# Windowed attention and two feed-forward layers on one core: granule 0's softmax normalized inside its transposition, and the opening planned anew

## The chip, the core and the metric

The kernel runs on one core of a Trainium2 chip. Its time is the device time of one execution in microseconds (us). The core's engines are TensorE (PE in the profile; PEld is its loading of weights), VectorE (DVE), ScalarE (ACT), GpSimd (POOL) and SyncE (SP), which here issues all the transfers (DMA).

## What is computed

The reference, cut to its core: attention for 2 batches of 8 heads, 768 tokens and 64 dimensions a head, in which a token sees its neighbours closer than 16 and 24 block summaries, then two feed-forward layers on the 1536 tokens.

```python
scores_l = scale * np.matmul(q, k.transpose(0, 1, 3, 2))     # only |i - j| < 16 is kept
scores_s = scale * np.einsum('bhsd,bhnd->bhsn', q, k_sum) + np.log(block)
a = np.exp(scores_all - np.max(scores_all, axis=-1, keepdims=True))
a = a / (np.sum(a, axis=-1, keepdims=True) + 1e-09)
attn_out = np.matmul(a, np.concatenate([v, v_sum], axis=2))  # k_sum: block max, v_sum: block mean
x = attn_out as [1536, 512]
h = x @ w_in;  x = (h * np.tanh(softplus(h))) @ w_out        # 512 -> 2048 -> 512
out = ((x @ w_a) * (x @ w_b)) @ w_out2                       # 512 -> 1536 -> 512
```

## The kernel before

The tokens are cut into six granules of 256, three to a batch. Heads are worked on in pairs (`p` 0 to 3, NP = 4), two heads side by side on the 128 partitions. For a granule and a pair the attention goes through these steps.

- `load_k`, `load_q`, `load_windows` and `prep_v` issue the transfers of keys, queries and values (all at L364); `prep_k` takes the block maxima of the keys on DVE (L462).
- `batch_s` makes the scores on PE: windows (L567, 64x96) and block summaries (L571, 64x24).
- `weights` is the softmax. DVE adds the mask and takes the minimum (L588, four times a pair), ACT takes the exponential with its sum (L594, four times), DVE adds 1e-9 (L597), takes the reciprocal (L599), and multiplies the 128x480 weights by it (L601).
- `batch_o` turns the weights over on PE (L626, four transpositions a pair), copies them out of PSUM on ACT or DVE (`copy`, L377 and L378; 120x512) and multiplies by the values (L638). Granule 0 alone adds the block values by a product of its own (L651), since its block means (L492, in `prep_v`, copied by `keep_v`) come late. The result is split into a rounded part (a CAST at L377 or L378) and a rest (L668).

The first feed-forward layer is done in `step1` for the first four chunks of 128 hidden units: `x_product` (L897), the activation Mish on ACT (L927), a rounded copy and a rest (L930 on DVE), and the product with `w_out` (L944). It starts on granule 0 while the other granules are still in the attention. All products of this kernel are made of three products of rounded parts. A chunk's weights come as 512 KB of 64-bit numbers and are converted by `load_w`: L688 on ACT, L693 and L696 on DVE, a CAST on ACT (L377) and the rest on DVE (L708). Later come the remaining chunks (L1076, L1121) and the second layer (L1076, L1229), which the change doesn't touch in the code.

No engine's order is written out. Every step is recorded in `Plan` by `Plan.add` with a key (the time at which it is due), the engines that may run it with a planned cost, and what it reads and writes. `Plan.emit` then plays the program through in planned time: at each moment each engine takes, of the steps whose inputs are there, the one with the smallest key; ACT adds `TABLE_PENALTY` to a step that needs another activation table than the one loaded (exp and Mish lie in different tables), PE adds `SHAPE_PENALTY` to a step whose products have another shape. The order so found is what each engine runs, and at run time each engine keeps it. So constants that only describe time (costs, due times, the model of the transfers) move instructions.

One more step has no part in the result: while PE has nothing to do early on, the plan puts in `fill`, a 128x512 bf16 product on zeros (L434) which keeps PE at work; eight stand at the start, and up to planned time `fill_end` more of them fill gaps. Once planned they run whether there is a gap or not.

## Time and profile before

| | us |
|---|---|
| median of 3 runs (lowest, highest) | 595.39 (595.28, 595.61) |
| the profiled execution | 595.54 |
| its span in the profile | 593.8 |

| engine | busy us | share of the span |
|---|---|---|
| PE | 586.6 | 99% |
| DVE | 489.2 | 82% |
| ACT | 318.8 | 54% |
| POOL | 6.7 | 1% |

The span runs from the first instruction to the last; 1.7 us of the profiled execution lie around it. The shares are means over stages: PE is busy throughout, DVE and ACT are nearly full from about 24 to 80 us and have slack afterwards. Times within the span are given from its start. The granted clock is the share of TensorE's full clock (2.4 GHz) that was granted in a stretch; its other level is half of that (1.2 GHz).

### The profile page before, as it was taken

The page shows a single profiled execution, that of the slowest core. Times are in us where ns is not written, and L with a number is a line of the kernel's source. Part 1 is how long each engine was busy: PE and PEld are TensorE (multiplying, and loading weights), DVE is VectorE, ACT ScalarE, POOL GpSimd, SP SyncE. Part 2 cuts the span into 40 slices and gives each one's busy share as a digit, 9 for nine tenths or more (in the row PEclk, how much of TensorE's full clock was granted, in tenths as well). Part 3 has the DMA queues.
Part 4 walks back from the last instruction along what each step waited for, and adds up shares of the span by engine and source line. Part 5 has one row for each costly group of instructions (what it writes and reads, how often), then busy time and mean ns, then how long its engine had stood idle before and what let it go on. Part 6 is the DMA issues. An engine that isn't in the chain of part 4 may idle for free.

```text
span 593.8 us, 10770 instructions
## 1 busy us (share of the span) xinstructions
PE 586.6 (99%) x4162; PEld 530.9 (89%) x4163; DVE 489.2 (82%) x1134; ACT 318.8 (54%) x711; POOL 6.7 (1%) x34
## 2 busy tenths in 40 slices
PE   9999999999999999999999999999999999999998
PEld 5788788889898899989999999999898999999896
DVE  6899999999999988979799998858686876855443
ACT  5699999457555555455376655444262434433030
POOL 3000000000000000000000000000000000000000
PEclk9899999999999999999999999999999999999999
DMA  9997700222233221222003133230122212300202
GB/s 282 348 345 221 224 20 3 71 72 72 71 107 106 73 71 72 72 71 72 0 1 100 43 107 111 103 107 20 52 72 71 108 35 72 107 0 2 89 18 107
DMA packets 22288, 54.89 MB, mean 92 GB/s; under 512 B 1917, under 2 KB 8061, under 8 KB 22237
## 3 DMA queue, kind: packets, MB, share of 16 engines
q1 hardware_dynamic: 22236, 54.21, 27.8%
q8 instruction: 32, 0.52, 0.4%
q14 instruction: 20, 0.16, 0.1%
HBM read 50.07 MB, written 3.15 MB: 90 GB/s over the span
## 4 chain that ended last, share of the span: by engine, by line
PE 92%; ACT 3%; DVE 3%; DMA 1%; issue 1%; ACTq 0%
PE bank L1076 44%; PE bank L1121 17%; PE bank L1229 17%; PE bank L944 5%; PE bank L897 4%; ACT attn L594 2%; PE bank L567 1%; PE bank L638 1%; DMA attn<-attn 1%; PE bank L626 1%; PE bank L434 1%; DVE attn L588 1%; ACT L927 1%; ACT rounded L377 0%; PE bank L571 0%
## 5 line engine op out<-in xcount | busy, mean ns | idle before, releaser
L1076 PE MATMUL bank<-rounded,wext 128*128 128x384 f32 x1176 | 213.8, 335 | 0.0
L1076 PEld LDWEIGHTS bank<-rounded,wext 128*128 128x128 f32 x1176 | 205.7, 188 | 3.5
L377 ACT CAST rounded<-arena 128x384 fp32r<-128x384 f32 (+2 forms) x145 | 80.8, 568 | 88.9 <-PE bank L1229 37.4
L1121 PE MATMUL bank<-rounded,wext 128*128 128x512 f32 (+1 forms) x456 | 104.7, 380 | 0.0
L1229 PE MATMUL bank<-wext,rounded 128*128 128x512 f32 (+2 forms) x441 | 100.0, 386 | 0.0
L1089 DVE TENSOR_TENSOR arena<-arena,bank 128x384 f32<-128x384 f32 x132 | 71.8, 550 | 31.2 <-PE bank L1076 23.1
L1229 PEld LDWEIGHTS bank<-wext,rounded 128*128 128x128 f32 x441 | 82.0, 188 | 16.3
L1121 PEld LDWEIGHTS bank<-rounded,wext 128*128 128x128 f32 x456 | 83.9, 188 | 12.6
L1085 ACT COPY arena<-bank 128x384 f32<-128x384 f32 x108 | 51.5, 478 | 56.5 <-PE bank L1076 53.8
L377 ACT CAST wext<-arena 128x512 fp32r<-128x512 f32 (+1 forms) x80 | 49.0, 621 | 33.2 <-PE bank L1076 12.7
L1076 PE MATMUL bank<-rounded 128*128 128x384 f32 x336 | 61.1, 335 | 0.0
L1076 PEld LDWEIGHTS bank<-rounded 128*128 128x128 f32 x336 | 58.5, 188 | 0.2
L1125 DVE TENSOR_TENSOR arena<-bank,arena 128x512 f32<-128x512 f32 (+1 forms) x76 | 49.9, 658 | 10.0 <-PE bank L1121 9.9
L1248 DVE TENSOR_TENSOR arena<-bank,arena 128x512 f32<-128x512 f32 (+2 forms) x37 | 25.0, 677 | 34.5 <-PE bank L1229 34.5
L708 DVE TENSOR_TENSOR wext<-arena,wext 128x512 fp32r<-128x512 f32 (+1 forms) x80 | 49.8, 639 | 0.7 <-ACT wext L377 0.3
L696 DVE SCALAR_TENSOR_TENSOR arena<-arena 128x512 uint32<-128x512 uint32 x68 | 46.6, 689 | 2.3 <-ACT arena L688 0.4
L708 DVE TENSOR_TENSOR rounded<-arena,rounded 128x384 fp32r<-128x384 f32 (+2 forms) x72 | 40.9, 583 | 4.8 <-ACT rounded L377 4.3
L594 ACT ACTIVATE attn<-attn 128x120 f32<-128x120 f32 x96 | 36.7, 386 | 7.6 <-DVE attn L588 7.5
L944 PE MATMUL bank<-rounded 128*128 128x512 f32 (+1 forms) x168 | 37.1, 367 | 0.0
L688 ACT ACTIVATE arena<-arena 128x512 f32<-128x512 f32 x38 | 25.8, 680 | 17.7 <-DMA arena<-in_w_out_dram 9.4
L897 PE MATMUL bank<-rounded 128*128 128x512 f32 (+1 forms) x168 | 35.3, 363 | 0.0
L897 PEld LDWEIGHTS bank<-rounded 128*128 128x128 f32 x168 | 28.1, 189 | 4.7
(75 smaller groups left out, 546.3 us busy)
## 6 DMA issues: line engine op xcount, KB each, us to landing
arena<-in_w_out_dram SPq DMA_DIRECT2D x28, 512.0 KB, 3.3
arena<-in_w_in_dram SPq DMA_DIRECT2D x16, 512.0 KB, 3.9
arena<-in_w_a_dram SPq DMA_DIRECT2D x12, 512.0 KB, 4.1
arena<-in_w_b_dram SPq DMA_DIRECT2D x12, 512.0 KB, 3.3
arena<-in_kT_dram SPq DMA_DIRECT2D x8, 384.0 KB, 9.6
out_dram<-arena SPq DMA_DIRECT2D x11, 256.0 KB, 2.0
attn<-in_qT_dram SPq DMA_DIRECT2D x5, 512.0 KB, 8.7
attn<-in_v_dram SPq DMA_DIRECT2D x3, 768.0 KB, 7.3
```

The lines of the kernel that those rows point to most:

```text
L377: alts = [("ACT", act_us(n), lambda env: nc.scalar.copy(out=dst(env), in_=src(env))), ("DVE", dve2_us(n) if fast else dve_us(n), lambda en ...
L594: act(key, SW + 90, lambda env, x=x: nc.scalar.activation(out=s[:, x, :], in_=s[:, x, :], func=AF.Exp, scale=-1.0, bias=negm[:, x:x + 1], ...
L696: dve(key, 512, lambda env: nc.vector.scalar_tensor_tensor(out=f.bitcast(U32), in0=hw.bitcast(U32), scalar=3, in1=f.bitcast(U32), op0=ALU. ...
L708: dve(key, n, lambda env: nc.vector.tensor_sub(out=r32(lo[0]()), in0=src, in1=hi[0]()), r=rd + hi[1], w=lo[1])
L897: nc.tensor.matmul(like(dst, b), lt, rt, start=(j == 0), stop=(j == 3 * KC - 1))
L944: nc.tensor.matmul(yp, lt, r32(rt), start=(fst and j == 0), stop=(lst and j == 2))
L1076: nc.tensor.matmul(dst, lt, r32(rt), start=(start and i == 0 and j == 0), stop=(last and i == 1 and j == 2), skip_group_check=True)
L1085: act(k, TN, lambda env: nc.scalar.copy(out=dst[0], in_=bank[env[nm[z]]][:, 0:TN]), w=[nm[z]] + dst[1])
L1089: dve(k, TN, lambda env: op(out=dst[0], in0=dst[0], in1=bank[env[nm[z]]][:, 0:TN]), w=dst[1] + [nm[z]], free=[nm[z]] if free else [])
L1121: nc.tensor.matmul(dst, lt, rt, start=(q == 0), stop=(q == 5))
L1125: dve(k + 1.2, n, lambda env: nc.vector.tensor_add(acc, bank[env[yn]][:, 0:n].rearrange(*shape[2], **shape[3]), acc), w=[yn] + ak, free=[yn])
L1229: nc.tensor.matmul(dst, lt, rt, start=(opens and j == 0), stop=(closes and j == n_mm - 1))
```

## The change

For granule 0 (`g < DG`, DG = 1) DVE no longer multiplies the weights by the reciprocal sums. GpSimd spreads the four reciprocals of a row into four diagonal 128x128 matrices (`affine_select` on a broadcast of `ri`, zero off the diagonal), and PE, in place of four transpositions, multiplies the weights by these diagonals: the product is the transposed and normalized block. The diagonals lie in the buffer that later takes the copy of the product. The other five granules are unchanged.

The rest are numbers of the planner: the model of the transfers, a later planned start of all engines, penalties for a change of table and of shape, the end of the fills, and due times of weights, values, queries and score batches. Cut to what matters:

```diff
-    SHAPE_PENALTY = 1.6
+    SHAPE_PENALTY = 2.37
-    DMA_LEAD, DMA_TAIL, DMA_RAMP = 0.62, 2.18, 8.0
+    DMA_LEAD, DMA_TAIL, DMA_RAMP = 0.62, 1.64, 8.0
+    START, RAMP = 0.8, ((2.8, 1.0), (7.3, 1.75), (11.0, 1.0), (1.0e9, 0.95))
-    TABLE, TABLE_PENALTY = 1.3, 5.37
+    TABLE, TABLE_PENALTY = 1.3, 16.96
...
-    pl.fill, pl.fill_end = fill, T0 + -7.99
+    pl.fill, pl.fill_end = fill, T0 + 3.64
...
-        dve(key, GU * SW, lambda env: nc.vector.tensor_tensor(
-            out=s, in0=s, in1=ri.unsqueeze(2).to_broadcast([P, GU, SW]), op=ALU.mult),
-            r=[("r", i)] + [("e", i, x) for x in range(GU)], w=sk)
+        if g >= DG:
+            dve(key, GU * SW, lambda env: nc.vector.tensor_tensor(
+                out=s, in0=s, in1=ri.unsqueeze(2).to_broadcast([P, GU, SW]), op=ALU.mult),
+                r=[("r", i)] + [("e", i, x) for x in range(GU)], w=sk)
+        else:
+            st["r", g, p] = (i, ri)
...
+            if g < DG:
+                i, ri = st.pop(("r", g, p))
+                diag = ar(ao, GU, P)
+
+                def diagonal(env, diag=diag, ri=ri):
+                    nc.gpsimd.affine_select(out=diag, in_=ri.unsqueeze(2).to_broadcast([P, GU, P]),
+                                            pattern=[[0, GU], [-1, P]], base=0, channel_multiplier=1,
+                                            compare_op=ALU.is_equal, fill=0.0)
+
+                def tr(env, s=s, name=name, diag=diag):
+                    for x in range(GU):
+                        nc.tensor.matmul(bank[env[name]][0:SW, x * P:(x + 1) * P], s[:, x, :], diag[:, x, :],
+                                         start=True, stop=True)
+
+                pl.add(key - 0.01, [("POOL", 0.71, diagonal)], r=[("r", i)], w=[sb(ao, GU * P)])
+                pe(key, 0.55, tr, words=16, duty=0.8, r=[sb(so, GU * SW)] + [("e", i, x) for x in range(GU)],
+                   w=[name, sb(ao, GU * P)], alloc=(name,))
...
-    w_dma = {("in", 0): -88.93, ("out", 0): -85.34, ("in", 1): -93.01}
+    w_dma = {("in", 0): -89.69, ("out", 0): -85.55, ("in", 1): -93.09}
-    BG, SP = (26.14, 40, 48, 59.27, 73.73), (0.5, 1.0, 1.0, 1.08, 1.43)
+    BG, SP = (26.14, 40, 48, 59.27, 73.73), (0.27, 1.0, 1.0, 1.0, 1.21)
-            bt[g, p] = 5.46 + 1.76 * p
+            bt[g, p] = 5.02 + 1.76 * p
-            kv, kd, ev = 9.86, -92.86, 1.5
+            kv, kd, ev = 7.38, -93.53, 1.5
```

What the numbers do is seen in the orders. In the changed file the lines up to 300 are 2 higher than before, those of `batch_o` and later up to 24.

**DVE, in granule 0's softmax, pairs 0 and 1.** 120 columns of scores in `bank` are masked (two instructions for one block), 128x24 are the block maxima of the keys, RECIPROCAL the reciprocal sums. Before:

```order
L588 ISA attn<-bank_64,attn 128x120
L588 ISA attn 128x1
L462 TENSOR_REDUCE attn<-arena 128x24
L597 TENSOR_SCALAR attn<-attn 128x4
L588 ISA attn<-bank_65,attn 128x120
L588 ISA attn 128x1
L599 RECIPROCAL attn<-attn 128x4
L588 ISA attn<-bank_64,attn 128x120
L588 ISA attn 128x1
L601 TENSOR_TENSOR attn<-attn 128x480
```

And now:

```order
L590 ISA attn<-bank_63,attn 128x120
L590 ISA attn 128x1
L599 TENSOR_SCALAR attn<-attn 128x4
L601 RECIPROCAL attn<-attn 128x4
L464 TENSOR_REDUCE attn<-arena 128x24
L590 ISA attn<-bank_64,attn 128x120
L590 ISA attn 128x1
L590 ISA attn<-bank_65,attn 128x120
L590 ISA attn 128x1
```

The multiplication is gone; the sum and the reciprocal of pair 0 stand ahead of the third reduction of keys (pair 2) and of all the masks of pair 1.

**PE, from the end of granule 0's scores to its block values.** 120x128 is the turning over of the weights, 64x64 the product with the values, 24x128 the block means, 64x256 the block values' product. Before:

```order
L638 MATMUL bank_63<-attn 64x64 x8
L626 MATMUL bank_64<-attn 120x128 x4
L492 MATMUL bank_65<-attn 24x128 x16
L638 MATMUL bank_68<-attn 64x64 x8
L626 MATMUL bank_66<-attn 120x128 x4
L492 MATMUL bank_65<-arena,attn 24x128 x8
L626 MATMUL bank_67<-attn 120x128 x4
L638 MATMUL bank_61<-arena,attn 64x64 x8
L492 MATMUL bank_65<-arena,attn 24x128 x8
L638 MATMUL bank_62<-arena,attn 64x64 x8
L651 MATMUL bank_68<-attn 64x256 x2
```

And now, where two fills stand right ahead of it:

```order
L436 MATMUL bank_66<-attn 128x512
L436 LDWEIGHTS attn
L436 MATMUL bank_67<-attn 128x512
L662 MATMUL bank_63<-attn 64x64 x8
L640 MATMUL bank_64<-attn 120x128 x4
L494 MATMUL bank_65<-attn 24x128 x16
L640 MATMUL bank_66<-arena,attn 120x128 x4
L494 MATMUL bank_65<-arena,attn 24x128 x8
L640 MATMUL bank_67<-arena,attn 120x128 x4
L662 MATMUL bank_68<-attn 64x64 x8
L494 MATMUL bank_65<-arena,attn 24x128 x8
```

The same steps, with the turning over of pairs 2 and 3 ahead of the values' products of pair 1. Of the fills behind the first eight, 7, 6, 2 and 3 stood between the four score batches and the first turning over; now 4, 3 and 2 stand between the batches and 2 behind the last, and the first turning over is put ahead of the third batch.

**SP, the transfers from the first `w_out` chunk on.** 128x4x256 are a granule's queries (here granule 2's), 128x2x512 values of batch 1. Before:

```order
L364 DMA arena<-in_w_out_dram 128x1024
L364 DMA attn<-in_qT_dram 128x4x256
L364 DMA arena<-in_v_dram 128x2x512
L364 DMA arena<-in_w_out_dram 128x1024
L364 DMA attn<-attn 24x4x512
```

And now:

```order
L366 DMA arena<-in_w_out_dram 128x1024
L366 DMA attn<-in_v_dram 128x4x256 x2
L366 DMA arena<-in_v_dram 128x2x512 x2
L366 DMA arena<-in_w_out_dram 128x1024
L366 DMA attn<-in_qT_dram 128x4x256
L366 DMA attn<-attn 24x4x512
```

The queries of granule 2 now stand behind the second `w_out` chunk and both halves of batch 1's values. On ACT the order holds 11 table loads where it held 15; the four that are gone stood in the stage in which the attention of granules 1 to 5 and the first layer overlap.

## Rows read from the trace of the kernel before

**Rows 1.** The page, part 1: the span, and PE's busy time.

```profile
span 593.8 us, 10770 instructions
...
PE 586.6 (99%) x4162; PEld 530.9 (89%) x4163; DVE 489.2 (82%) x1134; ACT 318.8 (54%) x711; POOL 6.7 (1%) x34
```

**Rows 2.** Windows by stage: length, busy PE, PEld, DVE, ACT, POOL; clock; DMA.

```profile
30.00:40.00 10.00, 8.85 (x225) 8.09 (x225) 9.59 (x37) 9.94 (x29) 0.52 (x1) 1.00 1.04 345
40.00:60.00 20.00, 19.61 (x345) 17.46 (x344) 19.57 (x82) 19.88 (x58) 0.00 (x0) 1.00 0.84 254
60.00:80.00 20.00, 19.42 (x263) 15.87 (x262) 19.69 (x79) 19.88 (x61) 0.52 (x1) 1.00 0.56 171
80.00:100.00 20.00, 20.00 (x298) 16.72 (x297) 19.46 (x73) 18.89 (x60) 0.00 (x0) 1.00 0.01 2
100.00:593.00 493.00, 490.98 (x2570) 453.21 (x2568) 397.89 (x767) 231.57 (x441) 0.00 (x0) 1.00 0.20 68
```

**Rows 3.** Windows of PE alone: length, busy PE, granted clock, DMA share, GB/s.

```profile
12.58:21.75 9.17, 8.71 (x163) 1.00 1.08 363
21.75:25.84 4.09, 4.09 (x130) 0.59 1.08 376
25.84:34.97 9.13, 7.56 (x139) 1.00 1.05 302
```

**Rows 4.** Timeline of DVE: start, duration, instruction (a reduction, a conversion, pair 3's multiplication).

```profile
8.49 0.95 DVE L462 TENSOR_REDUCE attn<-arena 128x24 f32<-128x768 f32 x1
...
15.96 0.70 DVE L696 SCALAR_TENSOR_TENSOR arena<-arena 128x512 uint32<-128x512 uint32 x1
16.57 0.65 DVE L601 TENSOR_TENSOR attn<-attn 128x480 f32<-128x480 f32 x1
```

**Rows 5.** Timeline of PE: fills, score batches, turning over, first product with w_out.

```profile
8.39 1.24 PE L434 MATMUL bank<-attn 128*128 128x512 bf16 x5 [0.16 <-DMA attn<-in_qT_dram]
9.56 0.40 PE L567 MATMUL bank<-arena,attn 64*64 64x96 f32 x8
...
11.89 0.40 PE L567 MATMUL bank<-arena,attn 64*64 64x96 f32 x8
...
15.54 0.39 PE L638 MATMUL bank<-attn 96*64 96x64 f32 x6 [0.19 <-issue]
...
17.37 0.62 PE L626 MATMUL bank<-attn 128*120 128x128 f32 x4 [0.18 <-ACT rounded L377]
...
30.42 0.40 PE L567 MATMUL bank<-arena,attn 64*64 64x96 f32 x8
...
34.97 1.68 PE L944 MATMUL bank<-rounded 128*128 128x256 f32 x12
```

**Rows 6.** The chain of waits: start, time on it, what.

```profile
12.71 1.22 DVE attn L588 x12
...
19.88 1.94 PE bank L651 x16
...
80.29 0.87 PE bank L626 x8
```

**Rows 7.** Timeline of ACT: sums of exponentials, granule 1's first exponential, a table load.

```profile
8.49 0.18 ACT L594 ACTIVATION_READ_ACCUMULATOR attn<-attn 128x1 f32 x1
...
15.14 0.18 ACT L594 ACTIVATION_READ_ACCUMULATOR attn<-attn 128x1 f32 x1
...
24.54 0.40 ACT L594 ACTIVATE attn<-attn 128x120 f32<-128x120 f32 x1 [1.70 <-DVE attn L588]
...
31.88 1.28 ACT L927 ACT_TABLE_LOAD   x1
```

**Rows 8.** GpSimd by form, 0 to 30 us: count, busy us, mean ns.

```profile
L401 POOL TENSOR_SCALAR_AFFINE_SELECT attn<-attn 64x288 f32<-64x288 f32 x2 | 0.9, 442 | 0.1
...
masks.py:199 POOL TENSOR_SCALAR_AFFINE_SELECT attn<-attn 128x128 f32<-128x128 f32 x1 | 0.3, 292 | 0.1
```

**Rows 9.** The page, part 6: transfers by line, KB each, median us to landing.

```profile
attn<-in_qT_dram SPq DMA_DIRECT2D x5, 512.0 KB, 8.7
```

More of the change, by code (lines that the diff above doesn't have):

```diff
@@ L108, in emit @@
         ready = {e: [] for e in engines}
-        free_at = {e: 0.0 for e in engines}
+        free_at = {e: self.START for e in engines}
         bank_free, where, held = {b: 0.0 for b in range(8)}, {}, set()
@@ L218, in emit @@
             if delay:
-                dma_free = max(dma_free, end + self.DMA_LEAD) + delay * (1.35 if 2.0 < dma_free < self.DMA_RAMP else 1.0)
+                dma_free = max(dma_free, end + self.DMA_LEAD) + delay * next(f for lim, f in self.RAMP if dma_free < lim)
                 end = dma_free + self.DMA_TAIL
@@ L273, in attention_mish_moe_bilinear_moe @@
     NEG = -1.0e9
-    T0 = 20.47
+    T0 = 20.27
     BITS64 = w_in.dtype != F32
@@ L305, in ar @@
         return a
+    DG = 1
     NQ, NSA, NAT, NST, NT, SPARE = 2, 4, 2, 3, 3, 832
@@ L622, in batch_o, with tr @@
             ats.append((p, ao, at))
-            def tr(env, s=s, name=name):
-                for x in range(GU):
-                    nc.tensor.transpose(bank[env[name]][0:SW, x * P:(x + 1) * P], s[:, x, :], ident)
-            pe(key, 0.48, tr, words=8, duty=0.83, r=[sb(so, GU * SW), sb(ident_o, P)], w=[name, sb(ao, GU * P)], alloc=(name,))
+            if g < DG:
[12 more added lines that the diff above has]
+                   w=[name, sb(ao, GU * P)], alloc=(name,))
+            else:
+                def tr(env, s=s, name=name):
+                    for x in range(GU):
+                        nc.tensor.transpose(bank[env[name]][0:SW, x * P:(x + 1) * P], s[:, x, :], ident)
+                pe(key, 0.48, tr, words=8, duty=0.83, r=[sb(so, GU * SW), sb(ident_o, P)], w=[name, sb(ao, GU * P)], alloc=(name,))
             copy(key, GU * P, lambda env, at=at: at[0:SW], lambda env, name=name: bank[env[name]][0:SW, :],
@@ L760, in attention_mish_moe_bilinear_moe @@
     size = lambda b: GT * len(gran2[b])
-    w_dma = {("in", 0): -88.93, ("out", 0): -85.34, ("in", 1): -93.01}
-    pace = (6.36, 5.0, 6.2, 6.0, 5.4)
+    w_dma = {("in", 0): -89.69, ("out", 0): -85.55, ("in", 1): -93.09}
+    pace = (6.36, 5.0, 6.11, 6.0, 5.4)
     att_in = {0: 4, 1: 8, 2: 8}
@@ L773, in attention_mish_moe_bilinear_moe @@
     slot_of = {kc: EW[i] for i, kc in enumerate((k, c) for c in range(NG1) for k in ("in", "out"))}
-    D1 = 15.29
+    D1 = 15.37
     seqL, tl = [], t
@@ L819, in attention_mish_moe_bilinear_moe @@
     for vi, b, c, ts, dt in steps1:
-        for kind, d in (("in", 0.0), ("out", 1.22 * dt)):
+        for kind, d in (("in", 0.0), ("out", 0.88 * dt)):
             first_use.setdefault((kind, c), ts + d)
@@ L843, in attention_mish_moe_bilinear_moe @@
         for p in range(NP):
-            kk, kd = (bt[g0, p] - 4.19, -100.0 + p) if b == 0 else (bt[g0, p] - 3.0, bt[g0, 0] - 6.96 + 0.5 * p)
+            kk, kd = (bt[g0, p] - 1.72, -100.0 + p) if b == 0 else (bt[g0, p] - 3.0, bt[g0, 0] - 6.96 + 0.5 * p)
             ev = end_s(g0 - 1) if b else 1.0
@@ L868, in need @@
         if (kind, c) not in w_at:
-            load_w(first_use[kind, c] - 7.48, kind, c, slot_of[kind, c])
+            load_w(first_use[kind, c] - 5.74, kind, c, slot_of[kind, c])
     def cut(offs, n, i=0):
@@ L1257, in expand @@
                 keep()
-    combine_x1(A_, t - 18.9)
-    combine_x1(B_, t - 1.27)
+    combine_x1(A_, t - 17.59)
+    combine_x1(B_, t - 3.23)
     done_l = set()
```

8 lines of the change are left out of this document (4 added, 4 removed).

## The prediction

> **What bounds the kernel now.** I read the page first, then windows by stage, then PE's, DVE's and ACT's timelines and the chain of waits in the first 35 us. PE is busy 586.6 us of a span of 593.8 [rows 1], so a change pays only where PE stands still, runs at half clock, or does work that isn't needed. The windows by stage [rows 2] show how little stands still: length less busy time is 1.15 us from 30 to 40, 0.39 from 40 to 60, 0.58 from 60 to 80, nothing to 100, and 2.02 in the 493 us behind that, which run far from the change. DVE and ACT are nearly full from 30 to 80, but PE has products to fill in, so it hardly notices.
>
> What is left is the opening. Three stretches of PE [rows 3] divide it. From 12.58 us (the last score batch of granule 0 is done) to 21.75 (granule 1's scores start) PE is busy 8.71 of 9.17: the stage is one of PE's own work, with two small pauses in it, 0.19 and 0.18 us [rows 5]. From 21.75 to 25.84 granule 1's scores run at a granted clock of 0.59 on average, so 4.09 x (1 - 0.59) = 1.7 us of them are lost to the half clock. From 25.84 to 34.97, the first product with `w_out` [rows 5], PE stands still 9.13 - 7.56 = 1.57 us; there it waits for a softmax that ACT paces: first exponential at 24.54, table load for Mish at 31.88 [rows 7], ACT without a longer pause in between. The sum is made in these three stretches.
>
> **Up to 12.6 us.** DVE loses four multiplications (0.65 each [rows 4]) and gains a wait: pair 0's sum now stands ahead of the third reduction of keys, and behind that all the masks of pair 1. The last of pair 0's four sums on ACT is read at 8.49 + 0.18 = 8.67 [rows 7], so after two short instructions the reduction starts at about 8.9 in place of 8.49 [rows 4]. Pair 0's diagonals start at 8.95 on GpSimd. That instruction isn't in the trace; the nearest have 288 and 128 elements a partition at 0.442 and 0.292 us [rows 8], a slope of 0.94 ns, which gives 0.65 for 512. Bounds: 0.44 (the longer row) and 4 x 0.292 = 1.17. At 0.65 the turning over of pair 0 runs at about 9.8 to 10.5, and the third score batch, now queued behind it, at 10.5 in place of 9.56 [rows 5]. Four masks of pair 1 (6 pairs of instructions take 1.22, so 0.2 each [rows 6]) and the fourth reduction follow: 8.9 + 0.87 + 0.8 + 0.87 = 11.45 (a reduction passes DVE on after some 0.87 of its 0.95). The last batch starts behind it and behind two fills, at about 11.8, against 11.89 before [rows 5]. So the wait is paid out of the fills, which are 11 where they were 18: -0.1 us, and the freed DVE time buys nothing here, since the exponentials set the pace. With the copy of pair 0's weights in the same place on ACT, the 16th sum ends at 15.2, against 15.14 + 0.18 before [rows 7].
>
> **From 12.6 to the block values.** Before, pair 3's multiplication ended at 16.57 + 0.65 = 17.22 and its turning over ran at 17.37 [rows 4, 5]. Now sum and reciprocal follow the exponentials directly and the diagonals are ready by 16.3, one us earlier. But PE is not free for them: it must do what it did before. New on PE are two fills (five take 1.24, so 0.25 each [rows 5]): +0.5. Three of the four products with diagonals lie here. Eight transpositions take 0.87 on the chain, so 0.44 for four [rows 6]. The products are f32, which the profile counts as two passes each; 16 passes of 256 columns take 1.94, 0.121 each [rows 6], so a pass of 128 columns lies between half of that and all of it, four products between 0.48 and 0.97. I take 0.50, by the columns: 3 x 0.06 = +0.2 (bounds 0.1 and 1.6). Of the two pauses the one ahead of pair 3's turning over goes, with some slack around it: -0.35. With the -0.1 from above the stretch ends 0.25 us later than before (bounds -0.5 and +1.6).
>
> Here a rule of the Trainium skill speaks against the change. In the trace no GpSimd instruction that reads runs beside a busy DVE in this stretch, so its price is not shown. The Trainium skill, SBUF — State Buffer, section Who interferes with whom, says that GpSimd shares a port pair with DVE, taken as a lock for a whole instruction by DVE instructions with two SBUF inputs or in a two-port mode. By it pair 3's diagonals would wait for the shift L693 that DVE starts right behind the reciprocal; I estimate 0.2 us more in the sum, since PE reaches that turning over only at about 16.6.
>
> **From the block values to 34.97.** The conversion of the first `w_out` chunk moves ahead of granule 0's last rest (L668) on DVE. It has a 0.70 us step [rows 4] and a shorter shift, and of these some 0.2 stick out behind what DVE waits for anyway: +0.2. It is then missing among granule 1's exponentials, where another conversion and a copy take its place on ACT, so from first exponential to table load ACT needs the same 7.3 us: nothing. So the first product with `w_out` comes 0.25 + 0.2 = 0.45 us later. Whether PE gets the half clock back doesn't count in this sum: its products would be done earlier and wait for ACT. The queries of granule 2 are now behind the second `w_out` chunk and 1 MB of values; I take it that they land by 30.4, where PE asks for them [rows 5].
>
> **Behind 35 us.** ACT has four table loads of 1.28 [rows 7] less, 5.1 us, in a stage where it is full. PE can win no more than it stands still there, 0.39 + 0.58 = 0.97 [rows 2]. I take 0.6 of it, bounds 0.97 won and 0.8 lost to a new wait in an order that is new throughout.
>
> **The sum.** +0.25 + 0.2 - 0.6 = -0.15, against the profiled execution: 595.54 - 0.15 = 595.4. That execution lies 0.15 above the median, so the runs should have a median of 595.2. About 0.2%, 1.2 us, is what a measurement of this kernel can tell from no change. So I forecast no change: the multiplication was on the chain of waits, but PE's own queue stood right behind it.
>
> **The rivals.**
>
> 1. *ACT's stretch shrinks.* If the exponentials of granule 1 start earlier instead of later (the fills fit into real gaps, and pair 3 being ready a us earlier lets PE close up), the 1.57 us of waiting before 34.97 goes for the most part. For it: the chain runs through DVE up to pair 3's multiplication. Against it: 8.71 busy of 9.17. It gives 595.2 - 1.4 = 593.8. Chance 0.17.
> 2. *The clock stays up* over granule 1's scores. Products take the place of transpositions in the stretch before, and that may count as more work. It is worth at most 1.7 us of PE, of which ACT's pace leaves perhaps 1.1: 594.1. Against it: the last thing before the fall is 1.94 us of L651 with 24 rows, unchanged. The Trainium skill, TensorE: Matmul & The Clock Gate, section Part 4: PE-mode transpose, says that transpositions do not count as PE work for the clock; by that the new products would. In this trace the clock stayed full over 12.58 to 21.75 with three sets of transpositions. Chance 0.08.
> 3. *The clock falls earlier: slower.* There are 18 fills between 5 and 12 us now and 11 afterwards (two of them behind the last batch), and PE waits some 0.8 us for pair 0's diagonals. If that is too little work, the clock is at half from about 12 us for a stretch like that in rows 3. There PE is the bound, so the 1.7 us lost there are lost in full: 596.9. It decides if the granted clock is under 1 anywhere between 9 and 16 us. Against it: the clock held at 15 to 19 us without any fill. Chance 0.15.
> 4. *Granule 2's queries come late: slower.* Their transfer can be issued only behind the second `w_out` chunk, which waits for a staging buffer until about 23.5. With the 8.7 us that such a transfer took [rows 9] they land at 32.5, 2 us after PE asks; half is hidden behind the copy that the next step waits for anyway: 596.4. Against it: the queue ahead is some 2 MB at 370 GB/s, 6 us. Chance 0.12.
>
> That the change doesn't do what it says is no rival beyond the forecast, which already has the removed multiplication buy nothing.
>
> **The numbers.** Forecast 0.48. Faster by over 0.2%: rivals 1 and 2 and a little of the forecast's lower edge, 0.27. Slower: rivals 3 and most of 4, 0.25. The range takes in both sides, down to rival 1 and up to rival 3 with a little more for a dear diagonal: 593.7 to 597.0. The forecast's own range is 594.4 to 596.2.
>
> **What would show it.** Right: the last block of L651 ends at 21.9 to 22.3; PE busy about 9 of 9.3 us before it; the diagonals at 0.6 to 0.8 us; first L944 at 35.0 to 35.6; PE standing still less than 0.7 us from 40 to 80. Wrong: L651 done before 21.2, a clock under 1 before 20 us, a score batch that waits for queries at 30 us, or more than 1.5 us of waiting behind 35.

## The result, and the profile after

The changed kernel takes 599.89 us (median of 6 executions, 599.00 to 602.62) where the kernel before, in runs beside it, took 595.68 (6 executions, 595.28 to 596.36). The ratio is 1.0079, with a 95% interval from 1.0055 to 1.0103: slower, by 4.2 us, and outside the predicted range (593.7 to 597.0). The profiled execution took 599.85 with a span of 596.6, so 2.8 us of the 4.2 stand in its span; another 1.5 lie outside it, 3.25 us where the kernel before has 1.74. In its other five executions 1.7 to 3.6 us lie outside and the span is 597.1 to 600.2, so the traced execution is the one with the shortest span; two of the others had a mean granted clock of 0.994, with spans of 599.0 and 600.2. No trace shows what is done outside the span, and that part stays open.

In the changed kernel lines stand 2 further down, and from the transpositions on 24: L567 is L569, L588 is L590, L594 is L596, L626 is L650, L638 is L662, L651 is L675, L668 is L692, L693 is L717, L897 is L921, L927 is L951, L944 is L968, L1076 is L1100. New are the diagonals L634 and the products with them L640.

The page, part 1 (answers to [rows 1]):

```profile
span 596.6 us, 10772 instructions
...
PE 586.9 (98%) x4171; PEld 530.5 (89%) x4172; DVE 481.0 (81%) x1110; ACT 322.4 (54%) x727; POOL 9.3 (2%) x38
```

PE is busy as long as before, 586.9 us against 586.6. What grew is the time in which it stands: 596.6 - 586.9 = 9.7 where it was 7.2. In that sum a dearer turning over stands against fewer fills (18 for 25 in the traces) and granule 1's scores at full clock.

Windows over the same stages as [rows 3], cut where the same instructions start (length; busy PE, PEld, DVE, ACT, POOL; granted clock; DMA share; GB/s):

```profile
13.24:22.76 9.52, 9.52 (x170) 7.48 (x169) 6.50 (x19) 5.35 (x18) 1.79 (x3) 1.00 1.06 373
22.76:25.45 2.69, 2.61 (x131) 2.45 (x129) 2.66 (x8) 1.82 (x4) 0.00 (x0) 1.00 1.03 367
25.45:35.98 10.53, 8.09 (x141) 6.83 (x137) 10.01 (x56) 10.02 (x38) 0.00 (x0) 1.00 1.04 309
35.98:130.97 94.99, 93.71 (x1176) 79.39 (x1177) 92.35 (x305) 82.19 (x232) 1.03 (x2) 1.00 0.41 127
130.97:596.00 465.03, 462.35 (x2410) 428.65 (x2408) 362.17 (x691) 216.77 (x415) 0.00 (x0) 1.00 0.19 67
```

The first stretch has no pause left and is still longer. The second is 1.4 us shorter, at a full clock. The third gives that back: PE stands 10.53 - 8.09 = 2.44 us in it where it stood 1.57. So the first product with `w_out` comes at 35.98, 1.0 later than before, and the long stage (everything from the first L1076, now L1100, on) at 130.97, where the kernel before starts it at 129.46. PE's last product of the kernel before:

```profile
587.82 3.16 PE L1229 MATMUL bank<-wext,rounded 128*128 128x512 f32 x20
```

and of the changed kernel:

```profile
587.67 6.10 PE L1253 MATMUL bank<-wext,rounded 128*128 128x512 f32 x33
```

So the long stage takes 593.77 - 130.97 = 462.80 us up to there, against 590.98 - 129.46 = 461.52. Of the 2.8 us in the span 1.0 is made before the first product with `w_out`, 0.5 between it and the long stage, and 1.3 in the long stage.

PE's timeline (start, duration, instruction; in brackets the idle time before it and what ended it), to be read beside [rows 5]:

```profile
9.73 1.14 PE L640 MATMUL bank<-attn 128*120 128x128 f32 x8 [0.87 <-POOL attn L634]
10.79 0.40 PE L569 MATMUL bank<-arena,attn 64*64 64x96 f32 x8
...
12.02 0.40 PE L569 MATMUL bank<-arena,attn 64*64 64x96 f32 x8
...
15.93 1.13 PE L640 MATMUL bank<-arena,attn 128*120 128x128 f32 x8
16.99 0.64 PE L494 MATMUL bank<-arena,attn 128*24 128x128 f32 x16
...
21.80 1.03 PE L675 MATMUL bank<-arena,attn 24*64 24x256 f32 x8
22.76 0.40 PE L569 MATMUL bank<-arena,attn 64*64 64x96 f32 x8
...
25.45 3.12 PE L921 MATMUL bank<-rounded 128*128 128x256 f32 x24
30.93 1.28 PE L650 MATMUL bank<-attn 128*120 128x128 f32 x8 [2.35 <-DVE attn L590]
32.22 0.40 PE L569 MATMUL bank<-arena,attn 64*64 64x96 f32 x8
```

Four products with diagonals (8 passes) hold PE for 16.99 - 15.93 = 1.06 us. In the kernel before the four transpositions of pair 3 start at 17.37 [rows 5], and the next instruction of its PE timeline follows 0.56 behind:

```profile
17.93 0.69 PE L638 MATMUL bank<-arena,attn 96*64 96x64 f32 x16
```

So a set is 0.50 dearer. At 30.93 PE of the changed kernel has waited 2.35 us for granule 1's softmax. Why that is late shows on DVE, GpSimd and ACT:

```profile
16.15 0.64 POOL L634 TENSOR_SCALAR_AFFINE_SELECT arena<-attn 128x512 f32<-128x512 f32 x1 [1.38 <-DVE attn L601]
```

```profile
16.19 0.87 DVE L717 TENSOR_SCALAR arena<-arena 128x512 uint32<-128x512 uint32 x1
...
24.53 0.42 DVE L717 TENSOR_SCALAR arena<-arena 128x512 uint32<-128x512 uint32 x1
24.87 0.42 DVE L692 TENSOR_TENSOR rounded<-bank,rounded 128x256 fp32r<-128x256 f32 x1
25.20 0.68 DVE L720 SCALAR_TENSOR_TENSOR arena<-arena 128x512 uint32<-128x512 uint32 x1
25.80 0.41 DVE L692 TENSOR_TENSOR rounded<-bank,rounded 128x256 fp32r<-128x256 f32 x1
```

```profile
25.92 0.66 ACT L379 CAST rounded<-arena 128x512 fp32r<-128x512 f32 x1 [1.21 <-DVE arena L720]
26.51 0.40 ACT L596 ACTIVATE attn<-attn 128x120 f32<-128x120 f32 x1
...
33.92 1.28 ACT L951 ACT_TABLE_LOAD   x1
```

The steps of `w_out`'s conversion, L717 at 24.53 and L720 at 25.20, stand on DVE between granule 0's rests (L692). On ACT its cast stands ahead of granule 1's first exponential, and waits 1.21 us for L720. That exponential comes at 26.51, against 24.54 [rows 7]; the table load comes 2.0 us later too.

The groups of waits of PE behind the opening's first microseconds (us in total, times, longest):

```profile
PE bank L650 <- DVE attn L590: 2.4, 1, 2.4
...
PE bank L640 <- POOL attn L634: 0.9, 1, 0.9
PE bank L494 <- DMA attn<-in_v_dram: 0.8, 1, 0.8
PE bank L1100 <- ACT arena L1109: 0.5, 1, 0.5
```

### The profile page after: what moved, and what is told of

It reads as the page before. It is cut to its first block, busy times and chain, and to the rows that moved or that the text cites. A ratio compares the mean times of both kernels' runs of the same rounds, so it can differ in the third digit from the quotient of the medians.

```text
span 596.6 us, 10772 instructions
## 1 busy us (share of the span) xinstructions
PE 586.9 (98%) x4171; PEld 530.5 (89%) x4172; DVE 481.0 (81%) x1110; ACT 322.4 (54%) x727; POOL 9.3 (2%) x38
## 4 chain that ended last, share of the span: by engine, by line
PE 90%; DVE 5%; ACT 2%; DMA 2%; issue 1%; POOL 0%; SPq 0%; ACTq 0%; DVEq 0%
PE bank L1100 43%; PE bank L1145 17%; PE bank L1253 17%; PE bank L968 4%; PE bank L921 3%; PE bank L662 2%; DMA attn<-in_v_dram 2%; PE bank L569 1%; PE bank L650 1%; DVE arena L720 1%; PE bank L436 1%; ACT attn L596 1%; PE bank L640 1%; PE bank L494 1%; DVE attn L590 1%
## 5 line engine op out<-in xcount | busy, mean ns | idle before, releaser
L1100 PE MATMUL bank<-rounded,wext 128*128 128x384 f32 x1176 | 214.7, 335 | 0.5 <-ACT arena L1109 0.5
L1100 PEld LDWEIGHTS bank<-rounded,wext 128*128 128x128 f32 x1176 | 205.7, 188 | 4.7 <-ACT arena L1109 0.7
L379 ACT CAST rounded<-arena 128x384 fp32r<-128x384 f32 (+3 forms) x154 | 84.8, 565 | 83.5 <-PE bank L1253 37.0
L379 ACT CAST wext<-arena 128x512 fp32r<-128x512 f32 (+1 forms) x80 | 49.1, 623 | 31.6 <-PE bank L1100 14.7
L1100 PE MATMUL bank<-rounded 128*128 128x384 f32 x336 | 61.5, 335 | 0.0
L1100 PEld LDWEIGHTS bank<-rounded 128*128 128x128 f32 x336 | 58.4, 188 | 0.6 <-ACT arena L1109 0.2
L720 DVE SCALAR_TENSOR_TENSOR arena<-arena 128x512 uint32<-128x512 uint32 x68 | 46.8, 690 | 6.5 <-ACT arena L712 4.0
L732 DVE TENSOR_TENSOR rounded<-arena,rounded 128x384 fp32r<-128x384 f32 (+1 forms) x72 | 40.3, 582 | 4.0 <-ACT rounded L379 3.7
L596 ACT ACTIVATE attn<-attn 128x120 f32<-128x120 f32 x96 | 36.7, 385 | 6.7 <-DVE attn L590 6.7
L968 PE MATMUL bank<-rounded 128*128 128x512 f32 (+1 forms) x168 | 37.2, 367 | 0.2 <-DVE rounded L954 0.2
L921 PE MATMUL bank<-rounded 128*128 128x512 f32 (+1 forms) x168 | 34.9, 362 | 0.0
L1187 ACT ACTIVATE arena<-arena 128x384 f32<-128x384 f32 x36 | 18.9, 526 | 27.4 <-DVE arena L1113 27.4
```

The source lines that it names most:

```text
L379: alts = [("ACT", act_us(n), lambda env: nc.scalar.copy(out=dst(env), in_=src(env))), ("DVE", dve2_us(n) if fast else dve_us(n), lambda en ...
L596: act(key, SW + 90, lambda env, x=x: nc.scalar.activation(out=s[:, x, :], in_=s[:, x, :], func=AF.Exp, scale=-1.0, bias=negm[:, x:x + 1], ...
L720: dve(key, 512, lambda env: nc.vector.scalar_tensor_tensor(out=f.bitcast(U32), in0=hw.bitcast(U32), scalar=3, in1=f.bitcast(U32), op0=ALU. ...
L732: dve(key, n, lambda env: nc.vector.tensor_sub(out=r32(lo[0]()), in0=src, in1=hi[0]()), r=rd + hi[1], w=lo[1])
L921: nc.tensor.matmul(like(dst, b), lt, rt, start=(j == 0), stop=(j == 3 * KC - 1))
L968: nc.tensor.matmul(yp, lt, r32(rt), start=(fst and j == 0), stop=(lst and j == 2))
```

## The experiments

Each run has its own comparison with the kernel before on the same chip; the ratio to it, with its 95% interval, is what counts. Differences in us are taken from the two medians.

**The two parts, apart and planned anew.** `DG = 0` in the changed kernel (its numbers, the old normalization), and the diagonals put into the kernel before with its old numbers. The planner makes a new order for either.

```diff
-    DG = 1
+    DG = 0
```

> All numbers of the change, but granule 0 is normalized on VectorE and turned over by transpositions as before (DG = 0); the planner orders the program anew for that. If the new numbers are what costs the time (the conversion of the first w_out chunk ahead of granule 1's softmax, the new order behind it), the time stays with the change: 598.5 to 600.5 us. If the diagonals cost it (four products at 1.06 us in place of 0.5, a wait of 0.9 for GpSimd), it is back near the kernel before: 595 to 597.

> The kernel before with the diagonals alone, on the old numbers; the planner orders the program anew for that. If the new numbers cost the time: 595 to 597. If the diagonals cost it: 598 to 600.

Measured: 600.07 us, ratio 1.0074 [1.0057, 1.0091], for the new numbers without diagonals; 600.49, ratio 1.0074 [1.0059, 1.0089], for the diagonals with the old numbers. Each half alone costs as much as both. So this division tells nothing of the parts: each run has an order of its own, with waits at places of its own (1.5 us at 75.8 in the first, 2.6 at 26.5 in the second). From here on the order is held: what the planner has set stays, and single instructions are exchanged in it.

**The products replaced in the changed kernel's order.** Both leave granule 0's weights unnormalized; the second takes the same product with the identity, without a wait for GpSimd.

```diff
-  nc.tensor.matmul(bank[...], s[:, x, :], diag[:, x, :], start=True, stop=True)
+  nc.tensor.transpose(bank[...], s[:, x, :], ident)        # e3
+  nc.tensor.matmul(bank[...], s[:, x, :], ident, start=True, stop=True)   # e4
```

> The changed kernel in its own order, instruction for instruction, but the four products with diagonals are transpositions again: granule 0's weights stay unnormalized, GpSimd still makes the diagonals and nobody reads them. This takes away four times some 0.55 us of TensorE work and the wait for GpSimd, and nothing else. If the diagonals cost the time: granule 1's scores start 2 to 3 us earlier, at about 20, and the time is 596 to 597. If the order costs it, the conversions on VectorE and ScalarE ahead of granule 1's softmax become the bound and hold most of it: 598.5 to 599.5.

> The changed kernel in its own order, but the four products read the identity in place of the diagonals: granule 0's weights stay unnormalized, the products cost what they cost in the change, and only the wait for GpSimd is gone. If that wait counts, the third score batch starts at about 9.7 us in place of 10.8 and up to 0.9 us of the loss go: 599.0. If it is swallowed by the two fills and the reduction of keys that the last batch waits for anyway, the time stays: 599.5 to 600.

Measured: 599.36, ratio 1.0058 [1.0043, 1.0073], and 600.60, ratio 1.0081 [1.0060, 1.0101]. With transpositions PE reaches its product L921 at 23.79 in place of 25.45, and then waits 2.6 us for the same softmax. In the order of the changed kernel what PE saves it waits, and in e3's trace a half-clock stretch (0.50 over 31.43 to 38.25) lies behind that wait, which the changed kernel's trace doesn't have. Without the wait for GpSimd (e4) nothing is gained.

**The diagonals in the old order; the old normalization in the new one.**

```diff
 # the kernel before, its order kept
-  nc.vector.tensor_tensor(out=s, in0=s, in1=ri..., op=ALU.mult)     # granule 0
+  nc.gpsimd.affine_select(out=diag, in_=ri..., ...)                 # ahead of the product
-  nc.tensor.transpose(bank[...], s[:, x, :], ident)
+  nc.tensor.matmul(bank[...], s[:, x, :], diag[:, x, :], start=True, stop=True)
 # the changed kernel, its order kept: the reverse
```

> The kernel before, instruction for instruction in its own order (nothing is planned anew), with granule 0's four normalizations by VectorE (4 x 0.70 us) taken out, four diagonals made by GpSimd, and products with them in place of granule 0's four transpositions. Theory A, the loss has two parts, the dearer products (1.06 us for four where four transpositions took 0.44) and an order in which granule 1's softmax comes late: only the first part is here; three of the four products lie behind 12.6 us, so TensorE comes to granule 1's scores 1.0 to 1.8 us later, about as much is left behind 35 us, and the time is 596.5 to 597.5. Theory B, the diagonals by themselves cost all of it, whatever the order (as the second run could be read): 599 to 600.5. Theory C, only the order counts, and what the products cost is regained in the removed normalizations and fills: 595.3 to 596.0.

> The changed kernel in its own order, with granule 0's normalization done as before: in place of each of the four diagonals on GpSimd VectorE multiplies the weights by the reciprocal sums (0.70 us each), and the four products are transpositions again (0.44 us for four of them in place of 1.06). Theory A: the products' 4 x 0.6 us come off TensorE, but granule 1's softmax is still behind the conversion of the first chunk of w_out, so that TensorE's wait near 28 us grows as the work ahead of it shrinks (it was 2.6 us where transpositions stood in place with nothing multiplied): 598.5 to 599.5. Theory B, the diagonals cost all of it: 595.5 to 596.5. Theory C, the order alone: 599.5 to 600.5.

Measured: 596.57 against 595.80, ratio 1.0013 [1.0004, 1.0022], and 599.95, ratio 1.0062 [1.0047, 1.0078]. This is the division that the first two runs couldn't make: the diagonals cost 0.8 us in the old order (the lower edge of theory A), and the new order is 4 us slower without them (theory C). PE's timeline of the first shows where the 0.8 comes from:

```profile
16.49 1.13 PE L634 MATMUL bank<-arena,attn 128*120 128x128 f32 x8 [0.19 <-POOL arena L627]
17.55 0.64 PE L492 MATMUL bank<-arena,attn 128*24 128x128 f32 x16
...
23.00 0.40 PE L567 MATMUL bank<-arena,attn 64*64 64x96 f32 x8
```

Again 1.06 for four products; granule 1's scores start 1.25 later than before [rows 3], the first product with `w_out` 1.2 later, and the long stage 1.0, after which nothing is gained or lost. In the second run the wait moved elsewhere, as in e3, and the half clock came behind it (windows of PE alone: length, busy, clock, DMA share, GB/s):

```profile
47.00:51.40 4.40, 2.51 (x41) 1.00 1.03 337
51.40:54.80 3.40, 3.40 (x92) 0.54 0.50 173
```

There PE stood 1.9 us for values and then ran at about half clock in a stretch that is PE's own work.

**The conversion of `w_out` put back behind granule 1's softmax.** The planner's emissions are recorded, and those of the conversion are sent out later, at the places of the kernel before.

```diff
+  behind = {457: 124, 456: 132, 458: 125, 459: 144, 460: 136}   # step: sent behind this one
```

> The changed kernel in its own order, except that the five instructions that convert the first chunk of w_out (ScalarE's copy and cast, VectorE's shift, its two combining steps and its rest) come not ahead of granule 1's softmax but spread through it, at the places that they had in the kernel before. Theory A: granule 1's first exponential comes about 1.0 us earlier (25.5 in place of 26.5), TensorE's wait of 2.4 us ahead of granule 1's first transposition shrinks to 1.0 to 1.5, the first Mish table load comes by 33.2 in place of 33.9, and the time falls by 0.8 to 1.3, to 598.6 to 599.1. Rival: the wait is handed on to the next stage, which waits for the same conversions or tables anyway: 599.6 to 600.2.

> Both edits of the two runs before: the changed kernel's order with the old normalization and transpositions, and with w_out's conversion spread through granule 1's softmax. Theory A: both parts are gone but for the transfers' new order and the values' wait near 49 us (0.8 us): 596.5 to 597.5. If the order's loss lies elsewhere (theory C with another cause than this conversion): 599 to 600.

Measured: 605.98 and 605.05. This was a mistake in the edit: the next transfer into the same staging buffer stayed ahead of the conversion, which so waited for it and converted the next chunk's data in place of the first. ACT's timeline shows the price:

```profile
33.96 0.68 ACT L722 ACTIVATE arena<-arena 128x512 f32<-128x512 f32 x1 [5.48 <-DMA arena<-in_w_in_dram]
```

The edit was made again with that transfer (step 509) behind it as well; beside it the two due times of what feeds the long stage were set back, alone and together with it.

```diff
+  behind = {457: 124, 456: 132, 458: 125, 459: 144, 460: 136, 509: 136}   # e9, e10, e12
-    combine_x1(A_, t - 17.59)                                             # e11, e12
-    combine_x1(B_, t - 3.23)
+    combine_x1(A_, t - 18.9)
+    combine_x1(B_, t - 1.27)
```

> The changed kernel in its own order, except that the five instructions that convert the first chunk of w_out come spread through granule 1's softmax, as in the kernel before, and the next transfer into the same staging buffer is issued behind them. Theory A (the order loses because granule 1's softmax stands behind that conversion): granule 1's first exponential comes about 1.0 us earlier (25.5 in place of 26.5), TensorE's wait of 2.4 us ahead of granule 1's first transposition shrinks to 1.0 to 1.5, the next values are issued by 38.5 in place of 39.4 so that the wait of 0.8 us near 49 is gone, and the time is 598.0 to 599.0 where the changed kernel took 599.9. Rival: the wait is handed on to the next stage and the time stays at 599.6 to 600.2.

> The edit of the run before together with the old normalization and the transpositions in granule 0, all in the changed kernel's order. The old order with the diagonals was 0.8 us slower than the kernel before, so the diagonals are worth about 1 us. Theory A: 597.0 to 598.0. If the order's loss lies elsewhere: 599.5 to 600.

> The changed kernel with two numbers alone set back, the due times of the combinations that feed the long stage (18.9 and 1.27 before its start in place of 17.59 and 3.23); the order of the opening does not change, that of ScalarE and VectorE from about 100 us on does. The changed kernel lost 0.8 us near 139 us, where TensorE waits 0.45 us for ScalarE's copy behind a conversion, and 0.45 more further on. Theory: both come from these two numbers, and the time falls by 0.8 to 1.2, to 598.7 to 599.1. Rival: the late start of the long stage makes them, whatever the due times: 599.6 to 600.2.

> Two edits at once in the changed kernel, diagonals kept: w_out's conversion behind granule 1's softmax (with the transfer behind it) and the old due times for what feeds the long stage. If both readings hold, they add: 597.0 to 598.0, close to the old order with the diagonals (596.6). If only one does: 598.5 to 599.2. If neither: 599.6 to 600.2.

Measured, against 595.62: 599.86 (ratio 1.0067 [1.0054, 1.0080]), 599.00 (1.0053 [1.0041, 1.0065]), 600.12 (1.0067 [1.0052, 1.0083]) and 598.77 (1.0052 [1.0039, 1.0066]). In e9 the first exponential of granule 1 did come earlier (25.99, by 0.5 where 1.0 was expected). PE's wait in front of the first transposition fell to 1.75, but 0.62 now stands in front of the second, so the sum is what it was:

```profile
PE bank L660 <- DVE attn L614: 2.4, 2, 1.7
```

In e11 the wait of L1100 for ACT is gone, and the long stage takes 461.90 us in place of 462.80, but it starts 0.4 later. Neither edit alone moved the time, and theory A as it stood fell. Both together (e12), and the conversion with the old normalization (e10), lie some 1 us lower by the medians, with intervals that overlap the changed kernel's. Two things that stop a gain show in the traces. In e9 a half-clock stretch follows the waits (windows of PE alone, as above):

```profile
27.00:31.37 4.37, 2.62 (x21) 1.00 1.05 281
31.37:38.19 6.82, 6.20 (x106) 0.52 0.88 277
```

e10 has the same (0.50 over 31.40 to 38.20); the traces of the changed kernel, of e11 and of e12 have none. The other thing shows in e10, on PE:

```profile
30.55 0.62 PE L657 MATMUL bank<-attn 128*120 128x128 f32 x4 [0.81 <-DVE attn L614]
32.27 0.60 PE L579 MATMUL bank<-arena,attn 64*64 64x96 f32 x8 [1.09 <-DMA attn<-in_qT_dram]
```

Granule 2's scores (here L579) then wait for their queries. On SP the changed kernel issues that transfer as the second of these:

```profile
24.31 0.34 SPq L366 DMA_DIRECT2D arena<-in_w_out_dram  x1
24.69 0.44 SPq L366 DMA_DIRECT2D attn<-in_qT_dram  x1
```

and the kernel before long ahead of that `w_out` chunk:

```profile
17.33 0.37 SPq L364 DMA_DIRECT2D attn<-in_qT_dram  x1
...
23.61 0.34 SPq L364 DMA_DIRECT2D arena<-in_w_out_dram  x1
```

So two limits, the softmax and the queries, end together near 32 us, and in the changed kernel's own profile only the one that came last shows.

**Queries and conversion together.** The transfer of granule 2's queries (step 81) is sent ahead of the values, alone (e13), with the conversion (e14), with the old due times (e15), and with the old normalization (e16).

```diff
+  behind = {81: 24}                    # and the steps of e9 in e14, e15 and e16
```

> The changed kernel in its own order, except that the transfer of granule 2's queries is issued ahead of two transfers of values and one of w_out, at about 17.5 us in place of 24.69. Theory E (two limits end together near 32 us: granule 1's softmax, for which TensorE waits 2.4 us, and granule 2's queries, which land at the same moment): the softmax still ends last, granule 2's scores start at 32.2 as before the edit, and the time stays, 599.4 to 600.2. Rival F (the queries' place on the queue is the whole loss): 597.5 to 598.5.

> The same with w_out's conversion spread through granule 1's softmax as well (the run with that alone: 599.9). Theory E: with both limits gone granule 2's scores start at 31.0 to 31.6 in place of 32.2 to 33.0, and the time is 598.0 to 599.0. Rival F: as in the run before, no further gain from the conversion. Rival G (the loss is made behind 36 us, by the order of the values, of the visits and of the long stage's first products): 599.4 to 600.2 in both runs.

> The same with the old due times of what feeds the long stage as well (the run with the conversion and these alone: 598.8). Theory E: 597.0 to 598.0. Rival G: 598.5 to 599.0, no better than without the queries' edit.

> All of the order's edits together with granule 0 normalized by VectorE and transposed as before. Theory E: the diagonals' 0.8 us come off, 596.2 to 597.2, within 1.5 of the kernel before. Rival G: 597.8 to 598.6.

Measured, against 595.87: 599.62 (1.0065 [1.0045, 1.0086]), 598.59 (1.0042 [1.0027, 1.0056]), 598.36 (1.0036 [1.0022, 1.0051]) and 598.36 (1.0043 [1.0027, 1.0059]). The queries alone give nothing, the conversion alone gave nothing, and both together 1.0 us more than the queries alone: that is what theory E said of the time. It isn't proved by it: the intervals of e13 and e14 overlap, and granule 2's scores in the profile of e14 start at 32.01 and not by 31.6, since the transposition there still waits, for DVE's multiplication (2.4 us in all, as in e9). Nor does a gain show ahead of the long stage: it starts at 131.48 in e14 and at 131.47 in e15, against 130.97 in the changed kernel. The old due times add 0.2, within the noise. And the diagonals' 0.8 us didn't come off in e16, against the expectation: PE there stands 1.2 us for the normalization, where e15 stands 0.9 for a diagonal, and 0.8 and 0.9 more near 23 and 33 us.

There is a rival that these runs don't exclude: the clock. At a mean granted clock of 0.999 or 1.000 the spans are 596.6 and 598.2 us in the changed kernel, 596.7 to 597.2 in e9, 596.9 and 597.2 in e14, and 596.2 to 596.5 in e15, so that little separates them there. At 0.994 they are 599.0 and 600.2 in the changed kernel, 597.9 and 598.4 in e9, and 597.1 to 597.7 in e10; no execution of e14 or e15 was at 0.994. So the medians may have come down because a wait went, or because the clock fell less often; with five or six executions of each this is not shown.

**A new plan with nothing to plan for.** What remains, 2.5 us, is spread over small waits. The last two runs plan the kernel before anew, with one cost or one number of the planner changed; both values are ones that the change itself writes.

```diff
-            pe(key, 0.48, tr, words=8, ...)                            # e17
+            pe(key, 0.55 if g == 0 else 0.48, tr, words=8, ...)
-    DMA_LEAD, DMA_TAIL, DMA_RAMP = 0.62, 2.18, 8.0                     # e18
+    DMA_LEAD, DMA_TAIL, DMA_RAMP = 0.62, 1.64, 8.0
```

> The kernel before, the same instructions and numbers, except that the planner takes 0.55 in place of 0.48 for each of granule 0's four transpositions (what the change writes for its products); it plans everything anew. Theory H (the order before is one that fits the chip, and any new plan loses some us to small waits, whatever the change meant): 598 to 600, with TensorE idle for 4.5 to 6 us in place of 3.2. Theory I (the change's own numbers lose it): 595.3 to 596.5, idle 3 to 4.

> The kernel before, the same instructions and numbers, except that the planner takes 1.64 in place of 2.18 for the tail of a transfer (one of the change's numbers, alone). Theory H: 598 to 600, as in the run beside it, though the number is another. Theory I: 595.3 to 596.5 if this number is harmless, and more only if it is one of those that lose.

Measured, against 595.88: 597.10 (ratio 1.0019 [1.0010, 1.0028]) and 597.45 (1.0025 [1.0016, 1.0033]). Both are slower by more than the noise, 1.2 and 1.6 us, though less than theory H asked (598). The page of the first, part 1, and its groups of waits:

```profile
span 595.9 us, 10764 instructions
...
PE 586.7 (98%) x4162; PEld 530.8 (89%) x4162; DVE 486.3 (82%) x1129; ACT 318.0 (53%) x714; POOL 6.7 (1%) x34
```

```profile
PE bank L626 <- DVE attn L601: 2.8, 4, 1.1
...
PE bank L567 <- DMA attn<-in_qT_dram: 0.6, 1, 0.6
```

The same work on PE, 9.2 us of standing in place of 7.2. So two plans of the same instructions, neither with the change's diagonals, lose that much. That any new plan would is not shown: two were tried, and with values of the change, so theory I (the change's own numbers lose it) isn't excluded either.

No version tried here beats the kernel before.

## Why the prediction was wrong, point by point

Three terms of the sum failed: the price of the product with a diagonal (+0.2, it was +1.5), the conversion ahead of the softmax ("some 0.2 stick out"), and, the largest, the gain behind 35 us (-0.6, it was +1.8 in the trace).

*What bounds the kernel.* Right in the main: PE's busy time is 586.6 to 586.9 in before, in the changed kernel, in e5, in e16 and in e17, and each loses by standing. In e6, e9 and e13, whose traces have half-clock stretches, it is 588.5 to 589.0. One reading was off: the 2.02 us behind 100 us are no waiting. PE's last product ends at 590.98 and the window at 593, so PE stood nowhere in the long stage.

*Up to 12.6 us.* Nearly right. A diagonal takes 0.64 (predicted 0.65), pair 0's turning over waits 0.87 for it, the third score batch comes at 10.79 (predicted 10.5), the last at 12.02 (predicted 11.8), and the fills swallow it.

*From 12.6 to the block values.* The term that failed is the price of the product: "I take 0.50, by the columns". It is 1.06, above even the upper bound of 0.97: a pass of 128 columns took 0.13 and not half of the 0.121 of a pass of 256. What sets this price no run separates; the eight loads of weights (PEld) beside such a set take 0.94 us, so that these loads may set it. The four transpositions that it replaces took 0.56 here and not the 0.44 of a later stage. So 3 x 0.50 = +1.5 in place of +0.2, near the term's own upper bound of 1.6. The two fills came (+0.5) and both pauses went (-0.4), and the products between took 0.7 less; granule 1's scores start at 22.76, 1.0 later, where 0.25 was forecast. The mark "the last block of L651 ends at 21.9 to 22.3" was missed: 22.83. The Trainium skill, SBUF — State Buffer, section Who interferes with whom, was weighed here: that GpSimd and DVE share a port pair. The traces agree that they collide. In the changed kernel it is the other way round: the diagonals stay at 0.64, and DVE's shift, which starts 0.04 behind one, takes 0.87 in place of 0.42. In e5 both pay, two diagonals with 1.84 us together and DVE's step with 0.83 in place of 0.69:

```profile
15.62 1.84 POOL L627 TENSOR_SCALAR_AFFINE_SELECT arena<-attn 128x512 f32<-128x512 f32 x2 [3.52 <-DVE attn L597]
```

```profile
16.14 0.83 DVE L705 SCALAR_TENSOR_TENSOR arena<-arena 128x512 uint32<-128x512 uint32 x1
```

*From the block values to 34.97.* "Some 0.2 stick out" failed. The conversion ahead of granule 0's last rest and of granule 1's softmax delayed the first exponential by 2.0 us, 1.0 of it beyond PE's own delay: its ACT step waits 1.21 us for its DVE step, and the exponentials queue behind it. With the conversion put back (e9) 0.5 of this went. That ACT's stretch keeps its length was right (26.51 to 33.92 is 7.4). The first product with `w_out` came 1.0 later, where 0.45 was forecast. The clock stayed up over granule 1's scores, 1.4 us, and the forecast was right not to count them: in e13, which has the changed kernel's softmax, it is at half there (0.50 over 24.14 to 27.55), PE comes to its product L931 (here L921) 1.4 later, waits 0.78 in place of 2.35, and turns granule 1 over only 0.12 later:

```profile
26.84 3.44 PE L931 MATMUL bank<-rounded 128*128 128x256 f32 x24
31.05 1.30 PE L660 MATMUL bank<-attn 128*120 128x128 f32 x8 [0.78 <-DVE attn L600]
```

Rival 4 was the second limit, hidden here behind the first: the queries, issued at 24.69 and not behind a "6 us" queue, land near 32 us (in e3 PE waits for them until 31.68, in e10 until 32.27), about where the softmax lets PE go on.

*Behind 35 us.* The sign failed: "-0.6" for four table loads. PE stands 94.99 - 93.71 = 1.28 us up to the long stage, against 94.49 - 93.52 = 0.97 in the same stretch before, whose window and waits were:

```profile
34.97:129.46 94.49, 93.52 (x1180) 1.00 0.42 133
```

```profile
PE bank L638 <- DMA attn<-attn: 0.5, 1, 0.5
PE bank L626 <- ACT arena L927: 0.4, 1, 0.4
```

So of the 0.97 only 0.4 was for ACT. That wait is gone, and a wait of 0.8 for values has come. The long stage, where nothing was forecast to change, took 1.28 more. One wait shows in it, 0.45 for ACT; with the old due times of what feeds it (e11) the wait is gone and 0.9 of the 1.28 with it. The sign "more than 1.5 us of waiting behind 35" came true: 1.28 + 0.45 = 1.73.

*The sum.* Every rival was priced for one place in the order, and the new order as a whole was priced only behind 35 us, at -0.97 to +0.8. The runs show 0.8 for the diagonals in the old order (e5), and +1.2 and +1.6 for new plans without them (e17, e18). e14 and e15 stand 1.5 and 1.7 us nearer to the kernel before than the changed kernel does. The three come near the 4.2, but the parts hide each other (e16 shows nothing for the diagonals) and the last is mixed with the clock, so the sum is no proof. What the changed kernel's trace loses beyond e5's lies behind the opening: e5 comes to the first product with `w_out` at 36.19, later than the changed kernel (35.98), and still has a span 1.8 us shorter. How much of the 4.2 lies in small waits, in half-clock stretches of executions that weren't traced, and outside the span stays open.

## What to carry to other kernels

When a change comes with a new order, measure it first in the old order, with the instructions exchanged in place: here that took the change's own price, 0.8 us, out of a loss of 4.2, which the two halves planned anew (4.5 and 4.9) could not. An order can be worth something by itself: here two new plans of the same instructions lost 1.2 and 1.6 us, and a forecast for a new order should allow for such a loss. Before a difference of 1 us is put down to a wait, the executions should be compared at the same granted clock. And where one wait is removed and the time stays, look for a second limit that ends at the same moment, on the transfer queue above all: what stands ahead of a late transfer there, and what that is waiting for.

## What the chip showed that was not expected

- An f32 product of 128 columns with 120 x 128 weights takes two passes of 0.13 us each, about as much as a pass of 256 columns with 24 x 64 weights (0.121, [rows 6]); a transposition of the same shape took 0.14 in all in the same stage.
- DVE's shift took 0.87 beside a diagonal of GpSimd and 0.42 without, and the diagonal kept its 0.64; in e5 two diagonals that met other steps of DVE took 1.84 together.
- In the executions of one and the same kernel the mean granted clock was 0.994 to 1.000, by half-clock stretches that some have and some don't. With the diagonals in the old order 9 of 11 executions ran at 1.000, beside 5 of 16 of the kernel before; the spans of those 5 were 593.8 to 594.9, not below the other eleven (593.4 to 594.9). The Trainium skill, TensorE: Matmul & The Clock Gate, section Part 4: PE-mode transpose, says that a transposition doesn't count as busy for the clock in the same way. These counts agree with that, but don't prove it: with the same products the changed kernel ran at 1.000 in 2 of 6 executions, and e17, with transpositions, in 6 of 11. The gain in time was nothing, because the next stage waits for the softmax.
- A half-clock stretch came behind a wait where PE was the bound (e6: 0.54 over 51.40 to 54.80, behind 1.9 us of standing), so that a wait there was paid for again, with up to 3.40 x 0.46 = 1.6 us of PE's time. In e9, e3 and e10 such a stretch is 6.8 us long. The changed kernel's trace has a wait of 2.35 us and no such stretch behind it.
